# State weights transposed as f16 pairs in 32-bit elements, with the first product's output rows written apart

## The chip, the cores and the metric

The kernel runs on one core of one Trainium2 chip. The metric is the device time of one execution in microseconds (us); the time of a kernel is the median of several executions. The core's engines each work through a queue of their own in a fixed order: PE (TensorE, matrix products, whose weight loads are shown apart as PEld), DVE (VectorE), ACT (ScalarE), POOL (GpSimd) and SP (SyncE, which here only issues transfers). SBUF is the working memory with 128 partitions; PSUM is the memory into which PE writes its products, and one of its banks holds 512 float32 numbers on each partition.

## The reference

Inputs are tokens `x` (8 batches, 8 heads, 512 tokens, 64 channels) and a `state` (8, 8, 32, 64). Cut to what matters:

```python
scores  = x @ state.T / sqrt(64);  a  = softmax(scores)    # 512 x 32 per head
xread   = a @ state                                        # tokens read the states
scores2 = state @ x.T / sqrt(64);  a2 = softmax(scores2)   # 32 x 512 per head
sread   = a2 @ x                                           # states read the tokens
y = concat(xread, sread)           # 544 rows per batch, heads side by side: 512 columns
h = y @ w_in                       # 512 -> 2048
g = max(h, 0) + alpha * min(h, 0)
out = g @ w_out                    # 2048 -> 512, float32, 4352 rows
```

## The kernel before

**The work.** Since `xread @ w_in` is `a @ (state @ w_in)`, the kernel multiplies states and `w_in` first. The step `m` (state_w_in) gives for a batch and a quarter f of the 2048 columns a tile `m` of 128 partitions (4 heads of 32 states), 2 groups g of heads and 512 columns. The transposed weights `aT` of the batch (128 partitions, 1024 f16 elements: 2 groups by 512 tokens) are then the moving operand of the **first product** (`F`, the function `first`, line 570): for each of 16 blocks jc of 128 columns it adds two matmuls, g = 0 and 1, each of 128x128 weights from `m` and 512 moving columns, into one PSUM bank `h` (128 columns of the layer by 512 tokens). With 7 batches this makes 7 x 16 x 2 = 224 matmuls; batch 0 has 28 more on the same line, since two of its blocks are made in halves by `first_part` (line 592). `negative` (`N`, ACT, line 623) and `prelu` (`G`, DVE, line 626) turn `h` into a tile `g`. POOL's `g_sum` (`U`, line 708) forms sums and differences of such tiles, and PE's `product` (`P`, line 729) multiplies `g` or the sums by parts of `w_out` or by sums of them (`W`, line 684, on POOL); `keep` and `quarter_out` (`K`, `Q`, lines 745, 760 and 762) bring the result out. Batch 0 has a simpler second product (`S`, line 640). The rows of `sread` are treated last as a ninth batch, whose first product is line 579.

**The weights.** For batches 1 to 7, PE computes the scores (`sc`, line 328) into two PSUM banks; DVE transposes them in blocks of 32x32 into the float32 tile `ts` (`sb`, line 360), finds the maximum (`smax`, line 393), POOL subtracts it (`ssh`, line 398), ACT takes the exponential (`sexp`, line 407), DVE sums (`ssum`, lines 416 and 417). `state_norm` (`snorm`, line 420) multiplies by the reciprocal sums and writes the f16 tile `an`: on POOL for batch 1 (`snorm.p.1`), on DVE for batches 2 to 7 (`snorm.v`). `weights_back` (`wb`, line 428, DVE) transposes `an` in 32x32 blocks into `aT`. Batch 0 goes another way (`at`, `ao`, over PE and ACT, lines 379 and 382).

**The order of elements.** A token of batches 1 to 7 is number 4p + 2j + r of its batch, with s = p its row among 128. `an` and `aT` stand in the order (r, j, g, s); `weights(b, g)` takes out the group g as (r, j, s), and `h` is written in that same order: `first` hands PE an output view whose elements follow one another without a gap. `g`, and all that comes after, is in the order (r, j, s) too.

**The order of the work** is written out by hand in the string ORDER, one token for a step (`F.3.12.0` is the first product of batch 3, block 12, in PSUM bank 0); each engine takes its instructions in the order in which the steps stand there. The tiles `an` and `aT` have two buffers each, `h` one of the single PSUM banks named in the token.

Of the kernel before, what the change touches and what calls it, by code (L numbers as in the profile page):

```python
# [7 lines left out]

F32 = mybir.dt.float32
F16 = mybir.dt.float16  # L10
EXP = mybir.ActivationFunctionType.Exp
COPY = mybir.ActivationFunctionType.Copy
RELU = mybir.ActivationFunctionType.Relu
ALU = mybir.AluOpType
# [87 lines left out]
def kernel(  # L102
# [17 lines left out]
    nc = tc.nc  # L120

    B, H, S, D = x.shape
    N = state.shape[2]
# [17 lines left out]
    def single(k, name, shape, dtype):  # L141
        return ps.tile(shape, dtype, name=name, tag=f"k{k}", bufs=1)
# [9 lines left out]
    def engine(e):  # L152
        return nc.gpsimd if e == "p" else nc.vector

    live = {}
# [3 lines left out]
    def load_x(b):  # L159
        xg = xgs[b] = att.tile([128, H, 2, 2, D], F16, name=f"xg_{b}", tag="xg", bufs=3)  # L160
        nc.gpsimd.dma_start(
            xg.rearrange("p k j r d -> p k j (r d)"),
            x[b].rearrange("k (p j r) d -> p k j (r d)", j=2, r=2),
        )


    def load_x0():
        xgs[0] = att.tile([128, H, 2, 2, D], F16, name="xg_0", tag="xg", bufs=3)
        for j in range(2):
            t = att.tile([128, H, 2, D], F32, name=f"x0_{j}", tag="ts", bufs=2)  # L170
            x0s.append(t)
        for e, j, first, last in (
            (nc.sync, 0, 0, 4), (nc.sync, 0, 4, 8), (nc.scalar, 1, 0, 4),
            (nc.scalar, 1, 4, 6), (nc.sync, 1, 6, 8),
        ):
            e.dma_start(
                x0s[j][:, first:last, :, :],
                x[0, first:last, 256 * j : 256 * (j + 1), :].rearrange("k (p r) d -> p k r d", r=2),
            )
# [21 lines left out]

    pattern = consts.tile([128, 256], F16)
    nc.gpsimd.iota(
        pattern, pattern=[[37, 256]], base=-4800, channel_multiplier=29,
        allow_small_or_imprecise_dtypes=True,
    )
    ident = consts.tile([128, 128], F16)
    make_identity(nc, ident)
    st = consts.tile([128, n_j, D], F16)

# [5 lines left out]

    w_in_sb = consts.tile([128, n_c, d_ff], F16)
    w_out_sb = consts.tile([128, n_jc, d_model], F16)
# [120 lines left out]
    def blocks(t):  # L339
        return t.rearrange("p (a n) -> p a n", n=N)  # L340

    def over_blocks(t):
        return t.unsqueeze(2).to_broadcast([128, t.shape[1], N])


    def cols(t, j, n):
        return t if j is None else t[:, n * j : n * (j + 1)]
# [57 lines left out]
    def state_exp(b, j=None):  # L405
        ts = cols(live["ts", b], j, S)
        nc.scalar.activation(ts, ts, EXP, bias=0.0, scale=scale)

# [8 lines left out]
        nc.vector.reciprocal(r1, r1)  # L417

    def state_norm(e, b, j=None):
        engine(e).tensor_tensor(  # L420
            blocks(cols(live["an", b], j, S)),
            blocks(cols(live["ts", b], j, S)),
            over_blocks(cols(live["r1", b], j, S // N)),
            ALU.mult,
        )

    def weights_back(b):
        nc.vector.transpose(live["aT", b], live["an", b])

    def weights(b, g):  # L430
        if b == 0:
            aT = live["aT", b].rearrange("p (j r g s) -> p r j g s", j=2, r=2, g=2)
        else:
            aT = live["aT", b].rearrange("p (r j g s) -> p r j g s", j=2, r=2, g=2)
        return aT[:, :, :, g, :]


# [13 lines left out]
    def token_exp(b, g):  # L451
        if ("e2", b) not in live:
# [6 lines left out]
            live["sc", b][:, :, :, g, :].rearrange("p r j s -> p (r j) s"),  # L459
            EXP,  # L460
            bias=live["nb", b][:, g : g + 1], scale=scale,
# [102 lines left out]
    def first(b, jc, k):  # L564
        w = S if b < B else B * N
        h = hs[b, jc] = single(k, f"h_{b}_{jc}", [128, w], F32)
        f, j = divmod(jc, 4)
        if b < B:
            for g in range(2):
                nc.tensor.matmul(  # L570
                    h.rearrange("p (r j s) -> p r j s", r=2, j=2),
                    ms[b, f][:, g, 128 * j : 128 * (j + 1)],
                    weights(b, g),
                    start=(g == 0),
                    stop=(g == 1),
                )
        else:
            for c in range(n_c):
                nc.tensor.matmul(  # L579
                    h,  # L580
                    w_in_sb[:, c, 128 * jc : 128 * (jc + 1)],
                    XS[:, c].rearrange("p q n b -> p (q n b)"),
                    start=(c == 0),
                    stop=(c == n_c - 1),
                )

    def first_part(b, pair, j, k):
        h = hs[b, pair, j] = single(k, f"h_{b}_{pair}_{j}", [128, 2, S // 2], F32)
        for i in range(2):
            f, n = divmod(2 * pair + i, 4)  # L590
            for g in range(2):
                nc.tensor.matmul(
                    h[:, i, :].rearrange("p (r s) -> p r s", r=2),
                    ms[b, f][:, g, 128 * n : 128 * (n + 1)],
                    weights(b, g)[:, :, j, :],
                    start=(g == 0),
                    stop=(g == 1),
                )
# [156 lines left out]
    def quarter_out(b, th, dh, e=None):  # L755
# [15 lines left out]
        "at": tokens_transposed, "ao": tokens_out,  # L771
        "sb": score_blocks, "smax": state_max, "ssh": state_shift, "sexp": state_exp,
        "ssum": state_sum, "smx": lambda e, b: state_max(b, None, e), "ssm": lambda e, b: state_sum(b, "s", e), "snorm": state_norm, "wb": weights_back,
        "tm": token_max, "nb": token_shift, "te": token_exp, "tsum": token_sum, "tn": token_norm,
        "tt": token_transposed, "rd": state_reads, "rdo": state_reads_out,
        "m": state_w_in, "mo": state_w_in_out,
        "F": first, "f": first_part, "n": negative_part, "g": prelu_part, "N": negative, "G": prelu, "S": second, "O": second_out,
        "Z": fill,
        "W": w_sum, "U": g_sum, "P": product, "K": keep, "Q": quarter_out,
# [34 lines left out]
```

## Time and profile before

| | |
|---|---|
| median of 3 runs | 209.19 us (208.65 to 209.2) |
| span of the profiled execution, first to last instruction | 209.0 us |
| instructions | 5033 |
| mean granted TensorE clock | 0.998 |
| HBM traffic over the span | 17.31 MB read, 8.91 MB written |

The profiled execution is known by its span; nothing else of its own time is on record, and the span stands within 0.1% of the median. In the profile, "busy" is the time in which an engine had an instruction of its own in work; matmuls overlap in PE's pipeline, so a group of matmuls is busy for less than count times mean duration. The chain of work that ended last is followed back from the last instruction to whatever released it. A row of a group gives line, engine, operation, output and input, shape and count, then busy us and the mean ns of one, then the idle time before it with what ended that.

### The profile page before, as it was taken

Reading aid. Unit: us, or ns where it says so; the run is one execution under the profiler, and the core shown is the slowest. Engines: PE = TensorE matmul, PEld = TensorE weight load, DVE = VectorE, ACT = ScalarE, POOL = GpSimd, SP = SyncE. Lnnn points to the kernel's source line nnn. Section 1 sums busy time; section 2 is a strip of 40 time slices with the busy share of each in tenths; the row PEclk is TensorE's granted clock in tenths of the full one; section 3 lists DMA queues with packets and bytes.
Section 4 is the critical chain, followed back from the end, with each engine's and each line's share of the span. In section 5 each row is a group of like instructions: output and inputs, shape, how many; then the busy total and the mean of one; then the engine's idle time right before and its main releaser. Section 6 shows DMA issues by size and latency. Waiting matters only on the chain.

```text
span 209.0 us, 5033 instructions
## 1 busy us (share of the span) xinstructions
PE 201.8 (97%) x1997; PEld 134.8 (65%) x1997; DVE 171.7 (82%) x251; ACT 155.6 (74%) x306; POOL 179.7 (86%) x113
## 2 busy tenths in 40 slices
PE   7899999998999999999999999999999999999992
PEld 2554343345556666678667765786877687788882
DVE  0688989999899999999999999999996967733231
ACT  4489999999999999987989968868855757603120
POOL 8149589987999899997997999887997999999960
PEclk9999999999999999999999999999999999999999
DMA  6999997984956799219886630126101200023223
GB/s 170 215 204 161 193 205 102 201 117 85 198 133 74 125 184 174 53 11 161 231 122 86 153 118 32 53 78 174 51 4 52 84 18 3 0 100 104 100 75 126
DMA packets 44038, 23.68 MB, mean 113 GB/s; under 512 B 22256, under 2 KB 43504, under 8 KB 44016
## 3 DMA queue, kind: packets, MB, share of 16 engines
q1 hardware_dynamic: 31152, 14.82, 28.3%
q0 software_dynamic: 11792, 8.09, 27.5%
q10 hardware_dynamic: 1072, 0.46, 0.9%
q8 instruction: 15, 0.25, 0.5%
q14 instruction: 7, 0.06, 0.1%
HBM read 17.31 MB, written 8.91 MB: 125 GB/s over the span
## 4 chain that ended last, share of the span: by engine, by line
PE 78%; DMA 7%; POOL 6%; ACT 4%; DVE 2%; issue 1%; SPq 0%; POOLq 0%
PE px L729 24%; PE h L570 21%; PE pv L729 13%; PE py L729 6%; POOL ws L684 5%; PE m_ps L521 4%; PE h L579 3%; DMA e2T<-e 2%; DMA xT<-xg 2%; DMA x<-in_x_dram 2%; PE fill L246 2%; PE sr_ps L494 2%; PE o L640 1%; ACT m L545 1%; POOL an L420 1%; PE sc L328 1%
## 5 line engine op out<-in xcount | busy, mean ns | idle before, releaser
L626 DVE SCALAR_TENSOR_TENSOR g<-neg,oma_sb,h 128x512 f16<-128x512 f32 (+1 forms) x142 | 93.9, 709 | 11.9 <-ACT neg L623 11.4
L623 ACT ACTIVATE neg<-h 128x512 f32<-128x512 f32 (+1 forms) x142 | 75.7, 580 | 16.6 <-PE h L570 11.5
L570 PE MATMUL h<-aT,m 128*128 128x512 f16 x252 | 66.8, 379 | 0.1
L729 PEld LDWEIGHTS <-gsum 128*128 128x128 f16 x480 | 46.6, 98 | 13.0 <-issue 0.9
L729 PEld LDWEIGHTS <-g 128*128 128x128 f16 x360 | 34.9, 98 | 9.0 <-issue 1.4
L708 POOL TENSOR_TENSOR gsum<-g,g 128x1024 f16<-128x1024 f16 (+1 forms) x16 | 32.2, 2012 | 5.5 <-DVE g L626 3.7
L570 PEld LDWEIGHTS <-m 128*128 128x128 f16 x252 | 23.8, 98 | 18.1 <-issue 1.8
L708 POOL TENSOR_TENSOR gsum<-g,gsum 128x1024 f16<-128x1024 f16 (+1 forms) x16 | 32.1, 2008 | 1.5 <-PE px L729 1.0
L708 POOL TENSOR_TENSOR gsum<-gsum,g 128x1024 f16<-128x1024 f16 (+1 forms) x16 | 32.1, 2009 | 1.0
L729 PE MATMUL px<-ws,gsum 128*128 128x256 f16 x240 | 32.1, 273 | 0.0
L708 POOL TENSOR_TENSOR gsum<-g 128x1024 f16<-128x1024 f16 (+1 forms) x16 | 32.0, 2011 | 0.0
L745 ACT COPY kept<-px 128x512 f32<-128x512 f32 (+1 forms) x24 | 13.6, 567 | 21.0 <-PE px L729 20.9
L547 ACT CAST m<-m_ps 128x512 f16<-128x512 f32 x35 | 19.2, 602 | 1.8 <-PE m_ps L521 1.5
L762 DVE TENSOR_TENSOR oq<-pv,kept 128x512 f32<-128x512 f32 (+1 forms) x16 | 10.4, 649 | 10.6 <-PE pv L729 10.4
L398 POOL TENSOR_TENSOR ts<-ts,mx 128x1024 f32<-128x1024 f32 x7 | 13.3, 1912 | 5.3 <-DVE mx L393 5.3
L729 PE MATMUL px<-w_out_sb,gsum 128*128 128x256 f16 x120 | 17.2, 273 | 0.0
L729 PE MATMUL px<-w_out_sb,g 128*128 128x256 f16 x120 | 17.2, 273 | 0.0
L729 PE MATMUL py<-w_out_sb,g 128*128 128x256 f16 x120 | 16.6, 273 | 0.0
L640 PE MATMUL o<-w_out_sb,g 128*128 128x512 f16 x64 | 16.4, 379 | 0.0
L729 PE MATMUL pv<-ws,gsum 128*128 128x256 f16 x120 | 16.4, 273 | 0.0
L729 PE MATMUL pv<-ws,g 128*128 128x256 f16 x120 | 15.9, 273 | 0.0
L545 ACT CAST m<-m_ps 128x1024 f16<-128x1024 f32 x13 | 13.3, 1023 | 0.4 <-PE m_ps L521 0.3
(75 smaller groups left out, 241.3 us busy)
## 6 DMA issues: line engine op xcount, KB each, us to landing
out_dram<-oq SPq DMA_DIRECT2D x28, 256.0 KB, 2.6
xg<-in_x_dram POOLq DMA_DIRECT2D x7, 512.0 KB, 7.0
w_in_sb<-in_moe_w_in_dram POOLq DMA_DIRECT2D x4, 512.0 KB, 8.5
w_out_sb<-in_moe_w_out_dram POOLq DMA_DIRECT2D x4, 512.0 KB, 12.9
out_dram<-osb SPq DMA_DIRECT2D x4, 256.0 KB, 3.5
x<-in_x_dram SPq DMA_DIRECT2D x2, 256.0 KB, 3.9
out_dram<-oq SPq DMA_DIRECT2D x4, 128.0 KB, 2.1
x<-in_x_dram ACTq DMA_DIRECT2D x1, 256.0 KB, 4.7
```

What stands on the lines that cost most here:

```text
L398: engine(e).tensor_tensor(blocks(cols(live["ts", b], j, S)), blocks(scored(b, j)), over_blocks(cols(live["mx", b], j, S // N)), ALU.subtract,)
L545: copier(e)(m_tile(b, f), t)
L547: copier(e)(m_tile(b, f)[:, g, :], t[g])
L570: nc.tensor.matmul(h.rearrange("p (r j s) -> p r j s", r=2, j=2), ms[b, f][:, g, 128 * j : 128 * (j + 1)], weights(b, g), start=(g == 0), ...
L623: nc.scalar.activation(neg, h, RELU, bias=0.0, scale=-1.0)
L626: nc.vector.scalar_tensor_tensor(g_tile(b, jc), negs.pop((b, jc)), oma_sb[:, jc : jc + 1], hs.pop((b, jc)), ALU.mult, ALU.add,)
L640: nc.tensor.matmul(outs[b, q], g_tile(b, jc)[:, 128 * q : 128 * (q + 1)], w_out_sb[:, jc, :], start=not begun and jc == 2 * jc2, stop=left ...
L684: engine(e).tensor_tensor(ws[i][:, rows, :], w_halves[a][:, rows, :], (ws[b] if b in ws else w_halves[b])[:, rows, :], ALU.subtract,)
L708: engine(e).tensor_tensor(t, x(), y(), op)
L729: nc.tensor.matmul(pbanks[b, name][:, i, :], of(b, c)[:, j, 128 * i : 128 * (i + 1)], moving[:, 4 * c + j, :], start=not begun and j == 0, ...
L745: copier(e)(t, pbanks[b, "x"])
L762: nc.vector.tensor_tensor(osb, pbanks[b, name], kept[b, add], ALU.add)
```

## The change

For batches 1 to 7, `state_norm` writes `an` in another order: the two rows r of a token pair side by side. The instruction reads `ts` and the reciprocal sums in three loops (r, a, n) and writes f16 elements with a step of two. `weights_back` gives the transpose both tiles as 32-bit elements, so it is an instruction of 512 elements a partition in place of 1024; two neighbouring f16 numbers move as one. `aT` then stands in the order (j, g, s, r), and the moving operand of the first product is read as (j, s, r). So that `h` remains in the order (r, j, s), `first` gives PE an output view in the order (j, s, r): consecutive columns of the product go in turn to the first and to the second half of the bank, 256 float32 numbers (1 KB) apart. Batch 0 is as before; no step of ORDER is moved, added or removed.

```diff
+U32 = mybir.dt.uint32
...
     def state_norm(e, b, j=None):
-        engine(e).tensor_tensor(
-            blocks(cols(live["an", b], j, S)),
-            blocks(cols(live["ts", b], j, S)),
-            over_blocks(cols(live["r1", b], j, S // N)),
-            ALU.mult,
-        )
+        an = blocks(cols(live["an", b], j, S))
+        ts = blocks(cols(live["ts", b], j, S))
+        r1 = over_blocks(cols(live["r1", b], j, S // N))
+        if b:
+            an = live["an", b].rearrange("p (a n r) -> p r a n", n=N, r=2)
+            ts = ts.rearrange("p (r a) n -> p r a n", r=2)
+            r1 = r1.rearrange("p (r a) n -> p r a n", r=2)
+        engine(e).tensor_tensor(an, ts, r1, ALU.mult)
 
     def weights_back(b):
-        nc.vector.transpose(live["aT", b], live["an", b])
+        nc.vector.transpose(live["aT", b].bitcast(U32), live["an", b].bitcast(U32))
 
     def weights(b, g):
-        if b == 0:
-            aT = live["aT", b].rearrange("p (j r g s) -> p r j g s", j=2, r=2, g=2)
-        else:
-            aT = live["aT", b].rearrange("p (r j g s) -> p r j g s", j=2, r=2, g=2)
+        if b:
+            aT = live["aT", b].rearrange("p (j g s r) -> p j g s r", j=2, r=2, g=2)
+            return aT[:, :, g, :, :]
+        aT = live["aT", b].rearrange("p (j r g s) -> p r j g s", j=2, r=2, g=2)
         return aT[:, :, :, g, :]
...
             for g in range(2):
+                if b:
+                    h_g = h.rearrange("p (r j s) -> p j s r", r=2, j=2)
+                else:
+                    h_g = h.rearrange("p (r j s) -> p r j s", r=2, j=2)
                 nc.tensor.matmul(
-                    h.rearrange("p (r j s) -> p r j s", r=2, j=2),
+                    h_g,
                     ms[b, f][:, g, 128 * j : 128 * (j + 1)],
                     weights(b, g),
```

## The prediction

> **What bounds the kernel now.** I read the page's shares of busy time first, then its chain of the work that ended last, then busy time by stretches.
>
> ```profile
> PE 201.8 (97%) x1997; PEld 134.8 (65%) x1997; DVE 171.7 (82%) x251; ACT 155.6 (74%) x306; POOL 179.7 (86%) x113
> ...
> PE 78%; DMA 7%; POOL 6%; ACT 4%; DVE 2%; issue 1%; SPq 0%; POOLq 0%
> PE px L729 24%; PE h L570 21%; PE pv L729 13%; PE py L729 6%; POOL ws L684 5%; PE m_ps L521 4%; PE h L579 3%; DMA e2T<-e 2%; DMA xT<-xg 2%; DMA x<-in_x_dram 2%; PE fill L246 2%; PE sr_ps L494 2%; PE o L640 1%; ACT m L545 1%; POOL an L420 1%; PE sc L328 1%
> ```
>
> ```profile
> 40.00:60.00 20.00, 19.37 (x232) 10.47 (x231) 18.94 (x26) 19.13 (x37) 17.94 (x12) 1.00 0.86 144
> 60.00:80.00 20.00, 20.00 (x254) 12.96 (x253) 19.86 (x28) 19.58 (x41) 19.16 (x11) 1.00 0.74 127
> 80.00:100.00 20.00, 20.00 (x192) 14.51 (x190) 19.69 (x29) 17.93 (x39) 18.66 (x11) 1.00 0.58 100
> 100.00:120.00 20.00, 19.91 (x251) 14.19 (x250) 19.68 (x26) 18.43 (x36) 18.41 (x11) 1.00 0.74 146
> 120.00:140.00 20.00, 20.00 (x176) 13.99 (x175) 19.59 (x29) 15.65 (x31) 18.34 (x11) 1.00 0.18 61
> 140.00:160.00 20.00, 20.00 (x214) 14.78 (x213) 18.55 (x28) 13.92 (x28) 17.30 (x9) 1.00 0.26 73
> ```
>
> The stretches list PE, PEld, DVE, ACT and POOL in that order, then the granted clock. From 40 to 160 us PE is busy without a pause, at full clock, and 78% of the chain is PE. DVE is nearly as full there, but it appears on the chain with 2%. So what lengthens a PE instruction in this stretch lengthens the kernel one for one, and what shortens a DVE instruction helps only where PE waits for DVE. Busy time could hide small gaps, since a matmul's record includes its way through the pipeline; the chain in order of time (start, duration, what) shows the true pace:
>
> ```profile
> 66.40 0.33 PE pv L729 x3
> 66.73 1.29 PE h L570 x6
> 68.02 0.44 PE px L729 x4
> ```
>
> ```profile
> L570 PE MATMUL h<-aT,m 128*128 128x512 f16 x252 | 66.8, 379 | 0.1
> ```
>
> Six first products take 1.29 us, so one every 0.215 us, or 0.42 ns for each of 512 columns. Four products of 256 columns take 0.44 us, 0.43 ns a column, and there is no gap between the pieces. The first products are therefore paced by their columns, not by their weight loads, and their 379 ns records overlap.
>
> **The change part by part.**
>
> *The transpose (line 428).*
>
> ```profile
> L428 DVE STREAM_TRANSPOSE aT<-an x7: 1222/1237/1245, 33.4 to 154.5; 128x1024 f16<-128x1024 f16 x7
> ```
>
> ```profile
> L360 DVE STREAM_TRANSPOSE ts<-sc 128x1024 f32<-128x1024 f32 x7 | 8.7, 1244 | 0.8 <-PE sc L328 0.8
> L286 DVE STREAM_TRANSPOSE alpha_sb<-alpha_rows 128x32 f32<-128x32 f32 x1 | 0.2, 202 | 0.0
> ```
>
> 1024 elements take 1237 ns as f16 and 1244 ns as float32, so the time goes by elements and not by bytes. Between 32 and 1024 elements of float32 it grows by 1042/992 = 1.05 ns per element; 512 take 202 + 480 x 1.05 = 706 ns. Each transpose saves 0.53 us, seven save 3.7 us of DVE.
>
> *What that is worth.* Who waits for DVE, from the waits of PE (PEld are PE's weight loads; us in total, times, longest):
>
> ```profile
> PEld L521 <- DVE g L626: 0.4, 1, 0.4
> PEld L570 <- DVE aT L428: 0.3, 1, 0.3
> PEld L640 <- DVE g L611: 0.3, 1, 0.3
> PEld L570 <- DVE r L467: 0.2, 1, 0.2
> PEld L570 <- DVE g L626: 0.2, 1, 0.2
> ```
>
> Together 1.4 us, of which the 0.3 us at line 640 belongs to batch 0, ahead of the first changed step (line 420 on POOL, at 29.3 us in the second fence under the sum). At most 1.1 us can come back. Beside a longer PE it comes to nothing: the same waits end earlier than PE arrives.
>
> *The norm (line 420).* It reads and computes as many elements, and writes f16 elements two apart.
>
> ```profile
> L420 DVE TENSOR_TENSOR an<-ts,r 128x1024 f16<-128x1024 f32 x6 | 7.3, 1213 | 0.1
> L420 POOL TENSOR_TENSOR an<-ts,r 128x1024 f16<-128x1024 f32 x1 | 1.9, 1915 | 0.5 <-DVE r L417 0.5
> L505 ACT CAST XS<-sr_ps 128x128 f16<-128x128 f32 x8 | 3.3, 489 | 0.2 <-PE sr_ps L494 0.2
> L745 ACT COPY kept<-px 128x512 f32<-128x512 f32 x21 | 12.5, 595 | 14.5 <-PE px L729 14.4
> L745 ACT COPY kept<-px 128x256 f32<-128x256 f32 x3 | 1.1, 373 | 6.5 <-PE px L729 6.5
> ```
>
> 1213 ns for 1024 elements is already about one element per ns, the pace of the transpose. The trace has no DVE write with a step. The lower bound is no cost. The upper one comes from line 505, where ACT writes f16 four elements apart: 489 ns for 128 elements, where the two copies of line 745 (0.87 ns per element between them) give 262 ns for gap-free ones; 1.77 ns more per element would be 1.8 us a norm. I take zero, since the norm's elements fall in consecutive 4-byte words, nearer to a gap-free row. If it is not zero it falls on DVE in six batches and on POOL in one, neither of which is the bound once PE grows.
>
> *The first product (lines 570 to 580).* Reading is the same in kind: gap-free runs of 128 f16 elements become runs of 256. Writing is new: no matmul of before writes neighbouring columns anywhere but side by side. Two neighbours now lie 1 KB apart in the bank. Its price per matmul has to be bounded. Lower end: nothing, 0.215 us stays. Upper end: the rows of this trace in which an engine goes from one PSUM element to one far off, each time. That is the copy of line 296, which reads `st_ps` with 256 bytes from element to element; beside it a gap-free copy.
>
> ```profile
> L296 ACT COPY stT<-st_ps 128x896 f16<-128x896 f16 x1 | 0.9, 907 | 0.4 <-PE st_ps L262 0.4
> L382 ACT COPY aT<-at_ps 128x512 f16<-128x512 f16 x2 | 1.2, 600 | 0.0
> ```
>
> They differ by 307 ns for 384 elements, 0.80 ns per element; 907 ns for 896 is 1.01 ns with the fixed part. So PSUM serves far-apart elements at least every 0.80 to 1.01 ns, and no row shows it serving them faster, while side by side PE fills one in 0.42 ns. At those paces 512 columns take 410 to 518 ns, 195 to 303 ns more than now. ACT's own pace may be what these rows show, so they bound the price and don't fix it. I take the point within them at which a pair of neighbours, now written together, becomes two writes: twice 0.215, that is 0.43 us, **0.215 us more per matmul**. This is an estimate and the step on which all hangs.
>
> [...]
>
> *The sum.* 224 matmuls x 0.215 us = +48.2 us on PE. What it can hide in: PE's gaps after the first changed product, at about 34 us.
>
> ```profile
> L570 PE MATMUL h<-aT,m 128*128 128x512 f16 x27 | 7.1, 380 | 0.1
> L640 PE MATMUL o<-w_out_sb,g 128*128 128x512 f16 x28 | 7.0, 379 | 0.0
> L521 PE MATMUL m_ps<-w_in_sb,stT 64*32 64x512 f16 x32 | 1.7, 385 | 0.0
> L328 PE MATMUL sc<-xT,stT 64*32 64x256 f16 x16 | 0.4, 274 | 0.0
> ```
>
> ```profile
> 29.30 1.92 POOL an L420
> ...
> 42.87 5.10 DMA e2T<-e
> ...
> 48.01 1.19 PE sr_ps L494 x64
> ...
> 60.80 0.34 PE m_ps L521 x8
> 61.14 0.61 PE sr_ps L494 x32
> 61.75 0.34 PE sc L328 x16
> ...
> 180.37 0.43 PE h L570 x2
> ```
>
> The first fence is all of PE between 33.4 and 48.0 us. By pace it is 27 x 0.215 + 28 x 0.215 + 32 x 0.042 + 0.34 = 13.5 us of 14.6, so 1.1 us of gaps, closed by the state reads that wait for a transfer until 48.0 us; they vanish when PE arrives later. From there to 180 us the chain is PE's but for one transfer between 100 and 120 us, beside which PE was busy 19.91 of 20 us. Net +47.1 us: 209.0 + 47.1 = 256.1, the profiled span; the median shown, 209.19, is as good as the span. The last changed product is at 180 us and the tail behind it moves along. **Forecast: 256 us**, its own range 248 (the 0.80 ns pace, and a few more us of waits closed) to 262.
>
> **The rivals.**
> *1. The bank takes a column every 0.42 ns wherever it lies* (the other side). Then PE is unchanged and DVE's 3.7 us decide. The relief acts where PE's loads wait for DVE, at most 1.1 us: 208.0 us or, with waits that only move to ACT or POOL, 209. It decides if six first products still take 1.29 us. For it: nothing in a matmul's present record depends on where `h` lies. Against: no row shows it. [...]
> *2. Part of the price* (only one of the two adding matmuls pays, or two places in the bank are held open at once): half is +24 us, less 1.1: 232 us.
> *3. More than double.* If a scattered element cost what line 505 shows, 1.77 ns more for each, a matmul would take 0.9 us more: 224 x 0.9 = +203 us, about 410. A third access for each column makes +96 us, 304. Little speaks for it, since line 296 passes at 1.01 ns in all.
> *4. The norm pays and the product doesn't:* six times 1.8 us less 3.7 us is +7.1 us of DVE; its idle time from 40 to 160 us is 3.7 us by the stretches, so some 3.5 us are late: 212.5 us.
> *5. The change doesn't do what it says:* a transpose whose time went by bytes stays at 1.24 us. Under the forecast that changes nothing; under rival 1 it leaves 209.2.
>
> **How the numbers follow.** Forecast 0.50; rival 2, 0.13; rival 3, 0.08; rival 4, 0.03; rival 1 with 5, 0.26, half of it a gain over 0.63 us (0.3%, about what a measurement of this kernel can tell from no change) and half within it. Slower: 0.50 + 0.13 + 0.08 + 0.03 = 0.74. Since rivals 1 and 5 hold 0.26, a range of 8 in 10 must reach down to them: 208 to 262, leaving out rival 3 and the ends.
>
> **What would show it.** Line 570's pace in the chain: 2.6 us for six if right, 1.29 under rival 1, about 1.9 under rival 2; its records longer by 0.2 us; lines 640, 579 and 729 unchanged. Line 428 at 0.70 us, line 420 at 1.21 on DVE. ACT's waits for `h` grow, and DVE, ACT and POOL lose in share. The forecast is wrong if line 570 keeps its pace, or if it slows and the chain shows PE waiting for something else.

## The result and the profile after

The changed kernel takes 256.02 us (median of 4, 255.93 to 256.14); in the same series the kernel before takes 209.19 us (208.65 to 209.84). The ratio is 1.223, with a 95% interval of 1.2194 to 1.2266: 46.8 us slower. The profiled execution has a span of 254.0 us and took 255.93 us, so about 1.9 us lie around the span.

Shares of busy time and the chain that ended last, of the changed kernel:

```profile
PE 247.8 (98%) x1997; PEld 142.3 (56%) x1997; DVE 173.9 (68%) x251; ACT 160.5 (63%) x306; POOL 179.6 (71%) x113
...
PE 91%; ACT 4%; DMA 2%; DVE 1%; issue 0%; ACTq 0%
PE h L577 40%; PE px L736 21%; PE pv L736 10%; PE py L736 5%; PE o L647 4%; PE m_ps L524 3%; PE h L586 3%; PE sr_ps L497 2%; DMA x<-in_x_dram 2%; ACT neg L630 1%; ACT m L548 1%; PE fill L247 1%; PE sc L329 1%; DVE g L633 1%; ACT m L550 1%; PE st_ps L263 0%
```

Line numbers have moved: the first product is line 577 (570 before), the norm 428, the transpose 431, the second product 736 (729). PE's busy time has grown by 46.0 us, almost all of the loss, and the first product's share of the chain from 21% to 40%. The other engines work as long as before within a few us and are only spread over a longer span. The pace, from the chain in order of time:

```profile
70.53 2.57 PE h L577 x6
73.11 0.44 PE px L736 x4
73.55 0.86 PE h L577 x2
74.40 0.44 PE px L736 x4
74.84 0.44 PE pv L736 x4
75.28 2.58 PE h L577 x6
```

Six first products take 2.58 us where they took 1.29; the second product's four stay at 0.44. All else of the change, and who now waits (groups, then the largest waits):

```profile
L577 PE MATMUL h<-aT,m 128*128 128x512 f16 x252 | 114.4, 595 | 0.1
L428 DVE TENSOR_TENSOR an<-ts,r 128x1024 f16<-128x1024 f32 x6 | 8.0, 1339 | 0.1
L431 DVE STREAM_TRANSPOSE aT<-an 128x512 uint32<-128x512 uint32 x7 | 4.9, 703 | 0.0
L428 POOL TENSOR_TENSOR an<-ts,r 128x1024 f16<-128x1024 f32 x1 | 1.9, 1917 | 0.5 <-DVE r L418 0.5
```

```profile
ACT neg L630 <- PE h L577: 49.3, 80, 2.6
DVE g L633 <- ACT neg L630: 47.5, 59, 2.4
```

The transpose takes 703 ns in place of 1237, as worked out. The norm on DVE takes 1339 ns in place of 1213, which was not foreseen. ACT, which waited 11.5 us for `h`, waits 49.3 us, and DVE behind it 47.5.

*Why the spans differ by 45.0 us and the medians by 46.8.* The two profiled executions don't start alike. These are pieces of the chain of the kernel before, then of the changed one:

```profile
7.43 0.66 PE fill L246 x2
...
9.45 1.30 PE fill L246 x5
...
13.40 0.67 PE m_ps L521 x16
```

```profile
6.79 0.34 PE fill L247 x2
...
8.20 0.97 PE fill L247 x5
...
11.83 0.67 PE m_ps L524 x16
```

The same two matmuls take 0.66 and 0.34 us, and the 16 products of states and `w_in`, the last thing before the kernel's body, begin at 13.40 and at 11.83 us. The difference has nothing to do with the change: in the twelve kernels below these products begin between 11.8 and 12.3 us or between 13.4 and 14.0 us, whatever is changed in them. It may be a good part of why executions of the kernel before range over 1 to 2 us, but only one of them has a trace, so that is not shown. From those 16 products to the end it is 195.6 us before and 242.2 after: **46.6 us**, in line with the medians. Why the starts differ the profile does not show: the granted clock stands at 1.00 in both. Below, "from the first products of states" means the span counted from there.

### The profile page after: what moved, and what is told of

It is laid out like the page before. It is cut to its first block, busy times and chain, and to the rows that moved or that the text cites. A ratio compares the mean times of both kernels' runs of the same rounds, so it can differ in the third digit from the quotient of the medians.

```text
span 254.0 us, 5033 instructions
## 1 busy us (share of the span) xinstructions
PE 247.8 (98%) x1997; PEld 142.3 (56%) x1997; DVE 173.9 (68%) x251; ACT 160.5 (63%) x306; POOL 179.6 (71%) x113
## 4 chain that ended last, share of the span: by engine, by line
PE 91%; ACT 4%; DMA 2%; DVE 1%; issue 0%; ACTq 0%
PE h L577 40%; PE px L736 21%; PE pv L736 10%; PE py L736 5%; PE o L647 4%; PE m_ps L524 3%; PE h L586 3%; PE sr_ps L497 2%; DMA x<-in_x_dram 2%; ACT neg L630 1%; ACT m L548 1%; PE fill L247 1%; PE sc L329 1%; DVE g L633 1%; ACT m L550 1%; PE st_ps L263 0%
## 5 line engine op out<-in xcount | busy, mean ns | idle before, releaser
L633 DVE SCALAR_TENSOR_TENSOR g<-neg,oma_sb,h 128x512 f16<-128x512 f32 (+1 forms) x142 | 97.8, 713 | 49.5 <-ACT neg L630 47.5
L577 PE MATMUL h<-aT,m 128*128 128x512 f16 x252 | 114.4, 595 | 0.1
L630 ACT ACTIVATE neg<-h 128x512 f32<-128x512 f32 (+1 forms) x142 | 78.5, 575 | 54.2 <-PE h L577 49.3
L736 PEld LDWEIGHTS <-gsum 128*128 128x128 f16 x480 | 49.2, 103 | 24.3 <-issue 19.1
L577 PEld LDWEIGHTS <-m 128*128 128x128 f16 x252 | 27.5, 113 | 33.7 <-issue 28.1
L736 PEld LDWEIGHTS <-g 128*128 128x128 f16 x360 | 36.2, 101 | 14.7 <-issue 10.9
L736 PE MATMUL px<-ws,gsum 128*128 128x256 f16 x240 | 32.9, 276 | 0.0
L752 ACT COPY kept<-px 128x512 f32<-128x512 f32 (+1 forms) x24 | 13.4, 560 | 22.7 <-PE px L736 22.6
```

Of the source, the lines that this page charges most:

```text
L577: nc.tensor.matmul(h_g, ms[b, f][:, g, 128 * j : 128 * (j + 1)], weights(b, g), start=(g == 0), stop=(g == 1),)
L630: nc.scalar.activation(neg, h, RELU, bias=0.0, scale=-1.0)
L633: nc.vector.scalar_tensor_tensor(g_tile(b, jc), negs.pop((b, jc)), oma_sb[:, jc : jc + 1], hs.pop((b, jc)), ALU.mult, ALU.add,)
L736: nc.tensor.matmul(pbanks[b, name][:, i, :], of(b, c)[:, j, 128 * i : 128 * (i + 1)], moving[:, 4 * c + j, :], start=not begun and j == 0, ...
L752: copier(e)(t, pbanks[b, "x"])
```

## The experiments

**Theory W**: the price lies in the writing alone; a first product takes 0.215 us when neighbouring columns stand side by side in the bank and 0.43 us when they stand apart. **Rival R**: the order of reading, or the 32-bit tile, costs. From e3 on the theory has a sharper form, **L**: the 0.215 us hold when each two consecutive columns fill 8 aligned bytes of the bank (an even float32 place and the odd one behind it), whatever lies between these pairs. "One write" in the expectations is the author's picture of it: the runs show what each pattern takes, not how the bank is written. The diffs of e1, e5 and e6 are against the changed kernel (e6 with the edit of e5), those of e11 and e12 against e5, all others against the kernel before. e1 was executed 9 times, e5 and e6 12 times each, every other one once; there the pace in the chain decides and not a time alone.

### e1: write side by side, read apart

```diff
-                if b:
-                    h_g = h.rearrange("p (r j s) -> p j s r", r=2, j=2)
-                else:
-                    h_g = h.rearrange("p (r j s) -> p r j s", r=2, j=2)
+                h_g = h.rearrange("p (r j s) -> p r j s", r=2, j=2)
...
-            return aT[:, :, g, :, :]
+            return aT[:, :, g, :, :].rearrange("p j s r -> p r j s")
```

> The changed kernel, but the product's output is written side by side again, in the order (r, j, s), and the moving operand is read from the same tile with a step of two f16 elements. The result is the reference's. Theory W (the writing alone costs, and the 32-bit transpose stands): six first products take 1.29 us again, line 428 keeps about 1.34 us and the transpose 0.70 us, DVE is 7 x 0.53 - 6 x 0.13 = 2.9 us less busy than before, and the time is 208.0 to 209.2 us. Rival R (the new order of the moving operand or the 32-bit tile costs): the pace stays between 1.9 and 2.6 us for six and the time between 230 and 256 us.

Measured: 210.74 us against 209.04, ratio 1.0076 (1.0049 to 1.0104). The 47 us are gone, though the 32-bit tile is still there, and the pace is far below the 1.9 to 2.6 us of Rival R. But the time is 1.7 us worse than before, not better, as theory W had it. The chain shows why:

```profile
60.84 0.98 PE px L733 x8
61.82 1.35 PE h L574 x6
63.17 0.44 PE px L733 x4
63.61 0.45 PE h L574 x2
```

Six take 1.35 us, not 1.29: 0.010 us more for each of 224 matmuls, 2.2 us. Reading with a step of two costs PE too, a twentieth as much as writing apart (e10 tries it alone).

### e2: write apart, and nothing else of the change

```diff
-                    h.rearrange("p (r j s) -> p r j s", r=2, j=2),
+                    h.rearrange("p (r c) -> p c r", r=2) if b else h,
```

> The kernel before, f16 transpose and norm as they were, but the first product of batches 1 to 7 writes its 512 columns in turn to the two halves of the bank (1 KB apart) without any change of what it reads, so that rows of h stand in other places. Theory W: six first products take 2.58 us, records of 634 ns, the time is 255 to 257 us. Rival R: 1.29 us, 209 us.

Measured: 256.03 us in one execution, within the 255.93 to 256.14 of the changed kernel, with the norm and the f16 transpose as they were.

```profile
64.32 0.86 PE h L570 x2
65.18 0.44 PE px L729 x4
65.62 1.72 PE h L570 x4
```

0.43 us each. Theory W holds: the view of the output alone makes the whole loss, and the faster transpose beside it is worth nothing that shows (242.1 us from the first products of states, 242.2 in the changed kernel).

### e3 and e4: what "apart" means

e3 writes two columns side by side and then jumps 1 KB; e4 never jumps far but leaves each second place free:

```diff
-                    h.rearrange("p (r j s) -> p r j s", r=2, j=2),
+                    h.rearrange("p (r c i) -> p c r i", r=2, i=2) if b else h,   # e3
+                    h.rearrange("p (c i) -> p i c", i=2) if b else h,             # e4
```

> The kernel before, but the first product of batches 1 to 7 writes two columns side by side (8 bytes, starting on a multiple of 8), then two in the other half of the bank, 1 KB away, and so on; rows of h stand in other places. Theory L (a pair that shares 8 bytes goes in one write, wherever the last one went): six first products take 1.29 us, 209 us. Rival H (each jump costs): half as many jumps, half the price, 1.94 us for six, about 232 us; if jumps between the halves cost in full, up to 256 us.

> The kernel before, but the first product of batches 1 to 7 writes with a step of two float32 numbers (8 bytes), first the even places of the bank and then the odd ones; rows of h stand in other places. Theory L: no two neighbouring columns share 8 bytes, so 2.58 us for six and 255 to 257 us. Rival D (the distance of 1 KB costs, two far places of one bank in turn): 1.29 us for six and 209 us.

Measured: e3 211.18 us, more than the 209 of theory L, but its first products of states began only at 13.95 us, and from there to the end it is 195.3 us, against 195.6 before; e4 255.97 us. The chain of e3, then of e4:

```profile
63.97 1.29 PE h L570 x6
65.27 0.44 PE px L729 x4
```

```profile
65.53 1.72 PE h L570 x4
67.25 0.44 PE px L729 x4
```

256 jumps of 1 KB in each matmul cost nothing when two columns are written at each stop (1.29 us for six); a step of 8 bytes costs as much as one of 1 KB (1.72 us for four, here and in e2). Rivals H (each jump costs) and D (the distance costs) both fall.

### e7 and e8: pairs on odd and on even places

Does any neighbour help, or only the one in the same 8 bytes? Both kernels write 508 columns in pairs in turn to the two halves, and fill the four places that are left with a second, small matmul; they differ in where the pairs start.

```diff
+                nc.tensor.matmul(
+                    halves[:, :, 1:255].rearrange("p r (c i) -> p c r i", i=2),   # e7; e8: 0:254
+                    w_g,
+                    live["aT", b][:, 512 * g : 512 * g + 508],
...
+                nc.tensor.matmul(
+                    halves[:, :, 0:256:255],                                      # e7; e8: 254:256
+                    w_g,
+                    live["aT", b][:, 512 * g + 508 : 512 * g + 512],
```

> The kernel before, but in the first product of batches 1 to 7 columns go in pairs in turn to the two halves of the bank as in e3, with each pair starting on an odd float32 number, so that it lies in two different 8-byte words; the four places left over at the ends of the halves are filled by a second matmul of four columns with its own weight load. Rows of h stand in other places. Theory L (aligned 8 bytes make one write): 0.43 us plus the small matmul's price; against e8, +224 x 0.21 = +47 us. Rival N (any two neighbours go together): the same time as e8.

> The control of e7: the same 508 columns in pairs in turn to the two halves, each pair starting on an even number, and the same small matmul of four columns. Both theories: 0.215 us plus the small matmul's price, which is a weight load and four columns, 0.02 to 0.1 us, so 214 to 231 us.

Measured: e7 262.25 us, e8 214.63. The difference is 47.6 us, or 46.5 from the first products of states. The matmuls of 508 columns in e7, then in e8:

```profile
L581 PE MATMUL h<-aT,m 128*128 128x508 f16 x224 | 110.2, 588 | 0.0
```

```profile
L581 PE MATMUL h<-aT,m 128*128 128x508 f16 x224 | 63.3, 376 | 0.0
```

Pairs side by side that start on an odd place pay in full, 588 ns a record where those on an even place take 376. The price follows theory L, and rival N (any neighbours) falls. The small matmul with its weight load costs 0.02 us (4.8 us for 224, from the first products of states), at the low end of what was expected.

### e5 and e6: nothing apart

e5 is the change without its price, the world of rival 1: norm, 32-bit transpose, gap-free reading, and columns written in the order of reading.

```diff
-                    h_g = h.rearrange("p (r j s) -> p j s r", r=2, j=2)
+                    h_g = h.rearrange("p (j s r) -> p j s r", r=2, j=2)
```

e6 makes that right by loading other tokens into the places and storing accordingly:

```diff
-            x[b].rearrange("k (p j r) d -> p k j (r d)", j=2, r=2),
+            x[b].rearrange("k (j p r) d -> p k j (r d)", j=2, r=2),
...
-            rows = "(j p r) d -> r p j d" if b == 0 else "(p j r) d -> r p j d"
-            return out[b * S2 : b * S2 + S, :].rearrange(rows, j=2, r=2)[th, :, :, cols]
+            rows = "(t i q) d -> t q i d"
+            return out[b * S2 : b * S2 + S, :].rearrange(rows, t=2, i=2)[th, :, :, cols]
```

> The changed kernel with its norm, its 32-bit transpose and its gap-free reading, but the product's columns are written side by side in the order in which they are read, (j, s, r), so that rows of h stand in other places. Nothing is apart any more, which is the case of rival 1 of the prediction: DVE 2.9 us less busy, PE's pace 1.29 us for six. Theory W: all of the 47 us was the writing and the relief is worth at most the 1.1 us in which PE's loads waited for DVE, so 208.0 to 209.1 us, a ratio of 0.995 to 1.000 to before. Rival: the stepped reading of e1 was not what made it slower than before but the norm or the 32-bit tile, and the ratio is again about 1.0076.

> As e5, but made right: batches 1 to 7 load token 256 j + 2 p + r where they loaded 4 p + 2 j + r, so that the order (j, s, r) is the order of the tokens, the halves of the second product are the halves j, and the output goes out in whole rows in order. The result is the reference's. The loads of x go in runs of 512 bytes in place of 1 KB. If the loads stay hidden: the time of e5, 208.0 to 209.1 us. If they come late (the page shows 7.0 us to landing, with some 30 us between the batches): no wait of PE on them in the profile, else up to 2 us more.

Measured: e5 208.77 us against 209.18, ratio 0.9983 (0.9966 to 0.9999); e6 209.08, ratio 1.0005 (0.9991 to 1.0019). The chain of e5 has the pace of the kernel before, so the change's own order of reading costs PE nothing:

```profile
61.33 1.29 PE h L577 x6
```

The relief of DVE by 2.5 us over the span is worth 0.4 us. In e6 that gain is within the noise of none. What differs from e5 is the load of x and the storing of the result. The groups of e5, then of e6, show POOL's time to give out one load:

```profile
L162 POOL DMA_DIRECT2D xg<-in_x_dram x7 | 6.5, 928 | 0.4 <-PE sr_ps L497 0.4
```

```profile
L162 POOL DMA_DIRECT2D xg<-in_x_dram x7 | 8.4, 1197 | 0.6 <-PE sr_ps L497 0.6
```

Shorter runs take POOL 0.27 us more per load, 1.9 us in all, on an engine that was 92% busy from 40 to 160 us in e5. The loads also land after 7.1 us in place of 6.0, but that says little: the 1 KB runs take 5.9 us in the changed kernel and 7.0 us in the kernel before. That POOL's 1.9 us take back the 0.3 us between e5 and e6 was not tried by itself. No version that is right and clearly faster than the kernel before was found.

### e9: the price where the chain still passes over ACT and DVE

```diff
-                    h.rearrange("p (r c) -> p c r", r=2) if b else h,
+                    h.rearrange("p (r c) -> p c r", r=2),
```

> As e2, but the 28 first products of batch 0 on the same line write apart too; rows of h stand in other places, of batch 0 as well. Theory W with the price on the path only where PE is the bound: these products run between 15 and 34 us, where the chain of the changed kernel passes over ACT and DVE until 28.5 us and holds 6 of them before that and 14 to 22 behind it, so between 6 x 0.215 = 1.3 and 28 x 0.215 = 6.0 us more than e2's 256.0: 257.3 to 262 us. Rival (the price is hidden at the start): 256.0 us, no change to e2.

Measured: 261.84 us, 5.8 more than e2 (5.5 from the first products of states). Even there nearly all of the 6.0 us lands in the time, although the chain of the changed kernel passes over ACT and DVE at the start. A chain names one path only; in the kernel before, PE was busy for 27.3 of the 28 us from 12 to 40 us.

### e10: the stepped reading alone

```diff
-                    weights(b, g),
+                    live["aT", b][:, 512 * g : 512 * (g + 1)].rearrange("p (c i) -> p i c", i=2)
+                    if b else weights(b, g),
```

> The kernel before, but the first product of batches 1 to 7 reads its moving operand with a step of two f16 elements, first the even and then the odd places of a gap-free run of 512, and writes side by side; rows of h come from other places of the tile. Theory S (the stepped reading alone made e1 slower): six first products take 1.35 us as in e1, 224 x 0.010 = 2.2 us more than before, 211.2 us. Rival (the 32-bit tile had to do with it): 1.29 us, 209.2 us.

Measured: 210.81 us; its one companion run of the kernel before took 210.99, so times don't decide here. The pace does:

```profile
61.95 1.35 PE h L570 x6
63.74 0.45 PE h L570 x2
```

The 1.35 us of e1 appear with the f16 tile as well: it is the step, not the 32-bit tile. From the first products of states the span is 1.3 us longer than before, so of the 2.2 us some 0.9 went into gaps of PE. That fits the weight loads of the state reads, which waited 0.9 us for a transfer before and have no such wait in e10.

### e11 and e12: the norm

```diff
-            an = live["an", b].rearrange("p (a n r) -> p r a n", n=N, r=2)
+            an = live["an", b].rearrange("p (r a n) -> p r a n", n=N, r=2)   # e11
+            an = live["an", b].rearrange("p (a n r) -> p a n r", n=N, r=2)   # e12; ts and r1 read as "p a n r" too
```

> e5 with a norm that writes its three loops without a gap, so that the pairs of the transpose hold other elements. If the step of two in the writing makes the norm's 1.34 us: 1.21 us again on DVE. If not, 1.34. The time 208.2 to 209.2 us either way.

> e5 with a norm whose innermost loop is the pair r: it writes without a gap and reads ts with a jump of 2 KB at each element. The values are those of e5. If a jump in reading costs DVE no more than the step in writing: 1.21 to 1.34 us. If each jump costs as a jump in PE's writing does, about twice: up to 2.3 us, and six of them, 6 us of DVE, would show as 209 to 212 us.

Measured: e11 210.56 us, above the 208.2 to 209.2 expected (its first products of states began late, at 13.94 us, and from there it is 194.7 us, against 194.8 in e5), and e12 209.61 us, inside the 209 to 212 expected if each jump costs; the rows tell what the jump itself costs. The norms of e11, then of e12:

```profile
L428 DVE TENSOR_TENSOR an<-ts,r 128x1024 f16<-128x1024 f32 x6 | 7.3, 1214 | 0.1
L428 POOL TENSOR_TENSOR an<-ts,r 128x1024 f16<-128x1024 f32 x1 | 1.9, 1914 | 0.5 <-DVE r L418 0.5
```

```profile
L428 DVE TENSOR_TENSOR an<-ts,r 128x1024 f16<-128x1024 f32 x6 | 7.4, 1234 | 0.1
L428 POOL TENSOR_TENSOR an<-ts,r 128x1024 f16<-128x1024 f32 x1 | 3.8, 3762 | 0.5 <-DVE r L418 0.5
```

The step of two f16 elements in the writing makes the norm's 0.13 us on DVE. A jump of 2 KB at each element read of `ts` costs DVE almost nothing (1234 ns), but on POOL the norm takes twice as long. The reciprocal sums are read with a jump of 64 bytes in e12, and the two jumps were not told apart.

## Why the prediction was right

**The bound.** It was taken from the stretches and the pace of the chain, and both bore out: PE stayed the bound (91% of the chain), and 48 us of longer matmuls gave 46.6 us of longer kernel. e2 repeats it without any other edit.

**The starting point of the sum was right by luck.** The 47.1 us were added to the span of 209.0 us as if it stood for the median of 209.19. But a span leaves out some 1.9 us of the time: the changed kernel's is 254.0 us, not the 256.1 that the sum gave for it, and the other executions of the kernel before whose span is on record have 206.6 to 209.1 us. The profiled execution of before was a late starter, and its first products of states at 13.40 us, some 1.6 us later than in the changed kernel, made up for most of what a span leaves out. Added to the median, the 47.1 us give 256.3, about as near to 256.02, so the forecast of 256 does not hang on it.

**The price per matmul.** 0.215 us more was forecast, 0.214 measured (2.57 to 2.58 us for six). The step that decided was an estimate between wide ends, with two supports. That a pair of neighbours is written together and becomes two writes was the author's estimate; no row of the kernel before and no run shows it. The runs show the doubling itself, and a condition that the prediction lacked: six first products take 1.29 us when each pair fills 8 aligned bytes (e3), four take 1.72 us when no pair does (e4), and the records last 588 ns with pairs on odd places against 376 on even ones (e7, e8). The other support, line 296, where ACT reads with 256 bytes between elements, tells nothing about PE's writing, and e3 and e4 show that distance plays no part. DVE makes the other copy of line 296 in 1084 ns, 1.21 ns per element, a row above the 1.01 that the prediction took for the upper end. That the doubling lies just above ACT's lower pace was luck: 0.84 ns a column against 0.80. Rival 1 (no price) is out by the pace: the same 512 columns take 0.43 us in e2. So are rival 2 (1.9 us for six) and rival 3.

**What hides it.** 1.1 us of gaps was forecast; 47.9 us (224 x 0.214) less 46.6 gives 1.3. The state reads waited for a transfer until 48 us before; in the changed kernel PE has no wait on that transfer.

**The relief of DVE.** 0.53 us per transpose was forecast, 0.534 measured; its worth without the price was put between nothing and 1.1 us, and e5 gives 0.4 us. So under rival 1 the time would have been about 208.8 us: a gain that lies within the 0.3%. The 1.1 us held as an upper end, but the list was not complete: it counted only what PE waits for DVE itself. In the profile of e5 two of those waits are gone, 0.5 us, and the weight loads' wait for the transfer ahead of the state reads has shrunk as well, from 0.9 to 0.2 us.

**The norm.** Taken at zero, it costs 0.126 us on DVE (e11 shows that the step in writing makes it) and nothing on POOL (1915 and 1917 ns). It was too small a term to matter beside the product, and rival 4's 1.8 us was far too high: ACT's line 505 is no measure for DVE.

**Rival 5**, that the transpose might not gain, fell with 703 ns.

## What to carry to other kernels

Where a matmul is paced by its columns, look at the output view before the input view. Here (f16, 512 columns, float32 output) it took 0.43 us in place of 0.215 when consecutive columns didn't fill 8 aligned bytes of the bank in pairs (e2, e4), while whole pairs jumped 1 KB within the bank for nothing (e3, 1.29 us for six). Where an engine with slack (DVE here) is relieved at the price of the engine that bounds the kernel, count the second first: 2.5 us of relief were worth 0.4 us, and the price was 47. When elements have to be re-ordered somewhere, compare by measured rows the places where it can be done. Here a step of two cost PE's writing 100% (0.43 us in place of 0.215, e4), PE's reading 5% (0.225 us, e10) and DVE's writing 10% (1339 ns in place of 1213), and a change of which token is loaded where cost 0.27 us of POOL's time a load.

## What the runs showed of the hardware that was not expected

- A first product whose moving f16 operand is read with a step of two elements takes 0.225 us in place of 0.215 (e1, e10).
- A norm that writes f16 with a step of two on DVE takes 1339 ns in place of 1213; on POOL the same step costs nothing (1917 ns against 1915). Reading `ts` with a jump of 2 KB at each element is the other way round: DVE 1234 ns, POOL 3762 in place of 1915 (e12).
- A matmul of four columns with its own weight load, behind one of 508 columns with the same weights, costs about 0.02 us (e8).
- The starts of the fourteen traces fall into two groups: the first products of states begin between 11.8 and 12.3 us or between 13.4 and 14.0 us. For differences under 1% the profiled spans have to be compared from there on.
